# Attention with a mixture of experts on Trainium2: token rows and gate logits out of one matrix product

## The chip, the cores and the metric

The kernel runs on one core of one Trainium2 chip. The metric is the device time of one execution in microseconds (us). Each core has TensorE (PE; its weight loads are shown as PEld), VectorE (DVE), ScalarE (ACT), GpSimd (POOL) and SyncE (SP, which issues DMAs).

## What is computed

```python
scores = scale * q @ k.T            # B=2, H=8, S=576, D=64, f32
# heads 0-3: 0 <= i-j < 32 ; heads 4-7: i >= j and i % 32 == j % 32
attn = softmax(where(mask, scores, -1e9))
x = (attn @ v) -> rows of 512      # 1152 tokens
logits = x @ w_gate                 # 8 experts
e = argmax(logits); gate = softmax(logits)[e]
out_e = relu(x @ w1[e]) @ w2[e]     # per token, experts of capacity 288
y = gate * out_e
h = y @ w_in; out = max(0.01*h, h) @ w_out
```

A token's place with its expert is its rank among the tokens of that expert.

## The kernel before, in words

**Stages.** First the attention with the choice of experts, then the experts (eight, in order of how full they are), then the last two layers. All engines work through lists whose order is written out by hand: the scheduler keeps each engine's order as the program states it.

**Units.** The attention is cut into 16 units (b, c, g): batch b, pair of heads c (c = 2 and 3 are strided heads, c = 0 and 1 local ones) and half g. In a batch the order is (2,0) (2,1) (3,0) (3,1) (0,0) (1,0) (0,1) (1,1). The steps of a unit are named by letters: 0 and 1 are the score products of its two heads (`stage_a`, L471), m the maximum and its subtraction (VectorE, L495), f or F the exp (ScalarE), s the sum and reciprocal (VectorE, three instructions), p the scaling (GpSimd), c the transposes of the weights (L523), e the two copies of them to SBUF (ScalarE, L531), d the product by V (L538) and x the copy of the result to `xT` (ScalarE, L554): features on the partitions, tokens along the row. t is a step that transposes q or k of a later unit and copies it (q in two copies, k in one).

**The loop.** `LOOP` (L23) has a line for each iteration `it`, with the order of the steps: unit `it` is in its steps 0, 1, m, f; unit `it`-1 in F, s, p; unit `it`-2 in c, e, d, x. The letters A, B and C advance the steps behind the units (`advance`, L736): every unit that completes a set of columns of `xT` puts a chain (L748) on a list, and the chain has a triple of actions for each following iteration, one for A, one for B, one for C.

**Behind the units.** Tokens are handled in tiles of 96. `logits` (L617) multiplies a tile of `xT` (stationary) by the 8 columns of the gate (`wg`, moving), for 3 or 6 tiles into one PSUM bank, and VectorE adds the result to `lga`. `rows` (L630) transposes three tiles of `xT` into a bank by the identity, and ScalarE copies them to `xra`, the rows of tokens. In a chain the products of `logits` stand at A and the add at B; `rows` stands at C of the next iteration, its transposes and its copy together; chains with six tiles have two such iterations. When the logits of 288 tokens are complete, `route_idx` (L639) finds their experts and ranks: five small VectorE operations, then ranking products on TensorE, then six more VectorE operations. `scatter` (L705) writes the rows to their places by an indirect DMA of GpSimd.

**Banks.** `bank_t` (L568) gives one of four PSUM banks with the tag T. It serves c (two banks), d, t, `logits`, `rows` and the ranking products. A bank is given out again when its last reader is done.

**The tail.** The last units, v = (1,0,0), w = (1,1,0), y = (1,0,1) and z = (1,1,1), and what is left of the chains are worked through by the string `TAIL` (L42): a step and a unit (`cw` is c of w, `mz0` is m of the first head of z), or a generator, advanced to its next yield. `Lk`, `Lv` and `Lw` are logits, `Rj` to `Rw` are rows, `Ly`, `Lz`, `Ry` and `Rz` the late forms for y and z, `i2` and `i3` the routing of the last two groups, `o` the order of the experts. `wg` is loaded by SP behind the attention's first loads (L723); at the start GpSimd clears `zt` (L379), `qz` and `ets` (L386).

Of the kernel before, what the change touches and what calls it, by code (L numbers as in the profile page):

```python
# [8 lines left out]
F32 = mybir.dt.float32  # L9
# [5 lines left out]
ALU = mybir.AluOpType  # L15
# [24 lines left out]


TAIL = """  # L42
sw ay0 pw ay1 cv my Rk Lk ev r1 dv xv az0 az1 Rk fy cw ew Lv Lk Rj dw cy Rj mz0 xw Lv Rv ey Rv Rl Lw Rl mz1 fz0
fz1 sy Lw i2 dy i2 cz0 xy i2 Rw i2 i2 cz1 sz0 ez0 i2 ez1 Ly i2 dz0 i2 Rw dz1 xz Ly i2 sz1 Ly i2 g5 Ry Lz Lz Lz
i3 i2 i2 i3 g6 i3 Rz Ry i3 Rz g7 wz1 i3 i3 Wy wz0 i3 i3 g8 i3 i3 g9 i3 i3 o g10 g11 G N
"""
FILL_AT = {3: (0, 1), 4: (2, 3), 5: (4, 5), 6: (6, 7)}
# [3 lines left out]
def kernel(ctx, tc, q, k, v, w_gate, w1, w2, w_in, w_out, out, cap):  # L51
    nc = tc.nc
    B, H, S, D = q.shape
    NT, DM = out.shape
    E = w_gate.shape[1]
# [3 lines left out]
    KD = DM // 128  # L59
    NF = FE // 128  # L60
    NG = FF // 128
    TT = 96
    TB = S // TT
# [13 lines left out]
    const = ctx.enter_context(tc.tile_pool(name="const", bufs=1))  # L77
# [145 lines left out]
    make_identity(nc, ident)  # L223
    identb = const.tile([128, 128], BF16, name="identb")
    nc.vector.tensor_copy(out=identb, in_=ident)
    wg = const.tile([128, KD, E], F32, name="wg")
    wgp = const.tile([128, 2, 2, E], F32, name="wgp")
    NI = S // STRIDE
    NR = RS // NI
# [12 lines left out]
    for t, off in ((slice(0, 1), 0), (slice(1, 3), STRIDE)):  # L242
        n = t.stop - t.start
# [119 lines left out]
    def run(gen, n=99):  # L363
        for _ in range(n):
            next(gen, None)

    with ExitStack() as actx:
# [7 lines left out]
            nc.gpsimd.memset(room[:, r:r + 1], float(2 * NT - WR[r]))  # L375
        index = xp.tile([1, E], F32, name="index")
        nc.gpsimd.iota(index, pattern=[[1, E]], base=0, channel_multiplier=0, allow_small_or_imprecise_dtypes=True)
        zt = wts.tile([TT, DM], F32, tag="tmp", name="zt", bufs=3)
        nc.gpsimd.memset(zt, 0.0)  # L379
        H2 = H // 2  # L380
# [187 lines left out]
        def bank_t():  # L568
            if tail[0]:
                tail[0] += 1  # L570
            return bank("S", 2)[:, 0] if tail[0] % 4 > 1 else bank("T")
# [5 lines left out]
        def late_logits(u):  # L577
            b, c, g = u
            pt = bank_t()
            lg = pt[:TT, :6 * E].rearrange("p (t h e) -> p t h e", t=3, h=2)  # L580
            for t in range(3):
                nc.tensor.matmul(lg[:, t], xT[b, c][:, (3 * g + t) * TT:(3 * g + t + 1) * TT], wgp[:, c],
                                 start=True, stop=True)
            yield
            lt = att.tile([TT, 3, 2, E], F32, tag="lt", name="lt", bufs=2)
            for h, r_ in inv(u):
                nc.vector.tensor_tensor(out=lt[:, :, h], in0=lg[:, :, h],
                                        in1=r_.to_broadcast([TT, 3, h.stop - h.start, E]), op=ALU.mult)
            yield
            dst = lga[b][:, 3 * g:3 * g + 3]  # L590
            for h in range(2):
                nc.vector.tensor_tensor(out=dst, in0=lt[:, :, h], in1=dst, op=ALU.add)
# [19 lines left out]
        def xra_of(r):  # L612
            if r not in xra:
                xra[r] = wts.tile([TT, 3, DM], F32, tag="xra", name="xra", bufs=3)
            return xra[r]

        def logits(b, c, t0, n):  # L617
            pt = bank_t()
            lg = pt[:TT, :n * E].rearrange("p (t e) -> p t e", t=n)
            for t in range(n):  # L620
                nc.tensor.matmul(lg[:, t], xT[b, c][:, (t0 + t) * TT:(t0 + t + 1) * TT], wg[:, c],
                                 start=True, stop=True)
            yield
            if c == order[0]:
                lga[b] = att.tile([TT, TB, E], F32, tag="lga", name="lga", bufs=1)
                nc.vector.tensor_copy(out=lga[b][:, t0:t0 + n], in_=lg)
            else:
                nc.vector.tensor_tensor(out=lga[b][:, t0:t0 + n], in0=lg, in1=lga[b][:, t0:t0 + n], op=ALU.add)

        def rows(b, c, t0):  # L630
            pt = bank_t()
            for t in range(3):
                nc.tensor.transpose(pt[:TT, t * 128:(t + 1) * 128],
                                    xT[b, c][:, (t0 + t) * TT:(t0 + t + 1) * TT], ident)
            yield
            nc.scalar.copy(out=xra_of(2 * b + t0 // 3)[:, :, c * 128:(c + 1) * 128],
                           in_=pt[:TT, :384].rearrange("p (t d) -> p t d", t=3))

        def route_idx(r):  # L639
            G = 3  # L640
# [75 lines left out]
        with tc.manual_schedule():  # L716
# [3 lines left out]
            load_vs(0, 1)  # L720
            load_ql(0, (1,))
            load_vl(0)
            nc.sync.dma_start(out=wg, in_=w_gate.rearrange("(c p) e -> p c e", p=128))  # L723
            for f in t_steps(0, order[0]):
                f()
            bg = []
# [20 lines left out]

            def chain(u):  # L748
                b, c, g = u
                if c >= H2 // 2:  # L750
                    lg = logits(b, c, 0, TB)
                    return [[lambda: run(lg, 1), lambda: run(lg)], [nop, nop, lambda: run(rows(b, c, 0))],
                            [nop, nop, lambda: run(rows(b, c, 3))]]
                lg = logits(b, c, 3 * g, 3)
                out = [[lambda: run(lg, 1), lambda: run(lg)], [nop, nop, lambda: run(rows(b, c, 3 * g))]]
                if c == 1:
                    r = 2 * b + g
                    idx, sc = route_idx(r), [lambda t=t: scatter(t) for t in range(3 * r, 3 * r + 3)]
                    out[1][1] = lambda: run(idx, 5)
                    out += [[lambda: run(idx, 1), lambda: run(idx)], [sc[0], nop, sc[1]], [sc[2], lambda: gate(r)]]  # L760
                return out

            def gate(r):
                route_gate(*st.pop(("rt", r)), slice(3 * r, 3 * r + 3), att)
# [14 lines left out]
            for it in range(NU - 2):  # L779
                us = todo.get(it, [])  # L780
                cur, prev = units[it], units[it - 1] if it else None
                for op in LOOP[it].split():
                    if op in "01":
                        stage_a(cur, int(op))
                    elif op in "ABC":
                        advance("ABC".index(op))
                    elif op == "t":
                        steps()
                    elif op == "m":
                        stage_m(cur)  # L790
                    elif op == "f":
                        exp_once(cur)
                    elif op == "F":
                        exp_once(prev)
                    elif op == "s":
                        if prev:
                            run(stage_s(prev))
                    elif op == "p":
                        if prev and prev not in late:
                            stage_p(prev, nc.gpsimd)  # L800
                    elif op == "L":
                        if it == 1:
                            load_qs(1)
                        fill(FILL_AT.get(it, ()))
                        if it == 5:
                            nc.gpsimd.memset(wgp, 0.0)
                            for par in range(2):
                                hp = slice(64 * par, 64 * par + 64)
                                nc.gpsimd.tensor_copy(out=wgp[hp, :, par], in_=wg[hp, :2])
                        if it == 6:  # L810
                            load_vs(1, 0)
                            load_vs(1, 1)
                        if it == 8:
                            load_ql(1)
                        if it == 10:
                            load_vl(1)
                        if it > 8:
                            load_whole(it - 9)
                        if it == NU - 3:
                            for j in range(2 * NE, 2 * NE + NW):  # L820
                                load_wide(j)
                    elif op in "cedx":
                        for u in us:
                            if op == "e":
                                stage_e(u, nc.scalar)
                            else:
                                {"c": stage_c, "d": stage_d, "x": stage_x}[op](u)
                for u in us:
                    if (u[1] < H2 // 2 or u[2] == 1):
                        bg.append(chain(u))  # L830
            bg.clear()
            last = dict(zip("vwyz", units[-4:]))
            gens = {"Lk": logits(1, 3, 0, TB), "Rj": rows(1, 2, 3), "Rk": rows(1, 3, 0), "Rl": rows(1, 3, 3),
                    "Lv": logits(1, 0, 0, 3), "Lw": logits(1, 1, 0, 3), "Ly": late_logits(y), "Lz": late_logits(z),
                    "Rv": rows(1, 0, 0), "Rw": rows(1, 1, 0), "Ry": late_rows(y), "Rz": late_rows(z),
                    "i2": route_idx(2), "i3": route_idx(3)}
            half = {"": both, "0": h0, "1": h1}
# [307 lines left out]
```

## Time and profile before

| what | value |
| --- | --- |
| median of 3 runs | 456.99 us (455.37 to 457.37) |
| profiled execution | 456.36 us, span 454.6 us |
| PE busy | 426.9 us, 94% of the span |
| DVE, ACT, POOL busy | 209.8, 158.5, 69.4 us |
| attention loop and tail | first 85 us or so of the span |
| experts | from about 100 to 234 us |
| last two layers | from 234 us to the end |
| mean granted TensorE clock | 0.974 of full speed |

The profile is of one execution, taken by the hardware. The span goes from the first to the last instruction; the execution's own time is 1.8 us more. A row of the timeline gives the start and the length of an instruction (or of several alike in a row, with their count), its engine, its line in the code, output and inputs; in square brackets stands how long the engine had been idle and what ended that. Matmuls overlap, so that the distance between the starts of two groups tells better than their lengths what one of them costs.

### The profile page before, as it was taken

What the parts mean: (1) busy time and instruction counts of PE and PEld (TensorE: products, weight loads), DVE (VectorE), ACT (ScalarE), POOL (GpSimd) and SP (SyncE); (2) the same over time, 40 slices, a digit from 0 to 9 for tenths busy, and PEclk for the clock granted to TensorE, in tenths of its full rate; (3) what the DMA queues carried; (4) which work ended last, traced back from release to release, by engine and by line L of the source; (5) the groups of instructions that cost most, each with busy time, mean ns of one, the idle gap of its engine ahead of it and who ended that gap; (6) DMA issues with size and microseconds to landing.
All of it is one profiled execution on the core that took longest, in us unless ns stands there. A gap on an engine that the chain in (4) does not pass through costs nothing.

```text
span 454.6 us, 7859 instructions
## 1 busy us (share of the span) xinstructions
PE 426.9 (94%) x2980; PEld 398.1 (88%) x2980; DVE 209.8 (46%) x472; ACT 158.5 (35%) x379; POOL 69.4 (15%) x127
## 2 busy tenths in 40 slices
PE   5999999159999999999999999999999999999994
PEld 5899999129999999999998989989988998998893
DVE  5677878849684442100002788773222233222220
ACT  4777776114232222211112443343322224322222
POOL 6353542730000000550000000000200000200002
PEclk9999999659999999999999999999999999999998
DMA  7999694369779999999980144200100000100001
GB/s 178 216 316 237 199 401 151 107 203 281 237 239 329 354 299 329 303 274 235 298 276 3 48 139 110 77 1 0 71 0 1 0 1 0 69 1 0 2 1 69
DMA packets 56487, 68.85 MB, mean 151 GB/s; under 512 B 20057, under 2 KB 36441, under 8 KB 56441
## 3 DMA queue, kind: packets, MB, share of 16 engines
q1 hardware_dynamic: 53403, 61.34, 44.8%
q0 software_dynamic: 1872, 4.73, 3.0%
q10 hardware_dynamic: 1166, 2.20, 1.7%
q8 instruction: 25, 0.41, 0.4%
q14 instruction: 21, 0.17, 0.1%
HBM read 60.38 MB, written 7.87 MB: 150 GB/s over the span
## 4 chain that ended last, share of the span: by engine, by line
issue 44%; PE 29%; POOL 2%; DMA 1%; POOLq 0%; SPq 0%
PE psS L898 14%; PE psL L905 14%; POOL out_dram L1114 2%; DMA tb<-tab 1%; PE psT L891 1%; PE psL L891 0%; POOLq L1141 0%; POOL gap L697 0%; SPq L123 0%; SPq L121 0%; POOLq L1114 0%; SPq L1060 0%
## 5 line engine op out<-in xcount | busy, mean ns | idle before, releaser
L905 PE MATMUL psL<-ht,pair 128*128 128x128 f32 (+6 forms) x512 | 79.8, 300 | 0.0
L898 PE MATMUL psS<-xe,pair 128*128 128x128 f32 (+6 forms) x512 | 79.2, 299 | 0.0
L898 PEld LDWEIGHTS psS<-xe,pair 128*128 128x128 f32 x512 | 73.0, 193 | 0.0
L905 PEld LDWEIGHTS psL<-ht,pair 128*128 128x128 f32 x512 | 70.7, 190 | 0.5
L1089 DVE TENSOR_TENSOR r<-psS,r 128x384 f32<-128x384 f32 x48 | 26.7, 557 | 82.6 <-ACT r L1088 82.6
L899 ACT ACTIVATE ht<-psS 128x128 f32<-128x128 f32 (+6 forms) x64 | 19.1, 301 | 102.1 <-PE psS L898 93.3
L1088 ACT ACTIVATE r<-psS 128x384 f32<-128x384 f32 x48 | 23.6, 492 | 86.7 <-PE psS L1086 86.6
L1114 POOL DMA_INDIRECT out_dram<-o,tb x9 | 8.7, 965 | 235.7 <-ACT o L1113 234.9
L914 DVE TENSOR_TENSOR yT<-psL,yT 128x128 f32 (+6 forms) x32 | 9.1, 321 | 74.2 <-PE psL L905 54.0
L1092 DVE TENSOR_TENSOR g<-r,g 128x384 fp32r<-128x384 f32 x48 | 26.8, 559 | 27.8 <-ACT g L1091 27.8
L1091 ACT CAST g<-r 128x384 fp32r<-128x384 f32 x48 | 24.6, 513 | 31.7 <-DVE r L1089 31.7
L1083 PE MATMUL psS<-yc,hle 128*128 128x384 f32 x72 | 24.5, 340 | 1.0 <-ACT yc L926 1.0
L490 PE MATMUL psS<-kT,qz 128*72 128x72 f32 (+1 forms) x224 | 24.8, 254 | 0.0
L1084 PE MATMUL psS<-yc,hle 128*128 128x384 f32 x72 | 24.4, 339 | 0.0
L490 PEld LDWEIGHTS psS<-kT,qz 128*72 128x72 f32 (+1 forms) x224 | 23.9, 160 | 0.0
L500 DVE TENSOR_REDUCE mx<-psS 72x8 f32<-72x576 f32 (+2 forms) x17 | 13.5, 795 | 8.1 <-PE psS L490 8.1
L1106 PE MATMUL psL<-hlx,g 128*128 128x512 f32 x42 | 16.6, 396 | 0.0
L1105 PE MATMUL psL<-hlx,g 128*128 128x512 f32 x42 | 16.6, 395 | 0.0
L1104 PE MATMUL psL<-hlx,g 128*128 128x512 f32 x42 | 16.3, 389 | 0.0
L1084 PE MATMUL psS<-yc,hlx 128*128 128x384 f32 x48 | 16.3, 340 | 0.0
L1084 PE MATMUL psS<-yc,hl 128*128 128x384 f32 x48 | 16.3, 340 | 0.0
L1083 PE MATMUL psS<-yc,hlx 128*128 128x384 f32 x48 | 16.1, 336 | 0.0
(309 smaller groups left out, 841.8 us busy)
## 6 DMA issues: line engine op xcount, KB each, us to landing
pair<-in_moe_w_dram SPq DMA_DIRECT2D x64, 512.0 KB
wide<-in_moe_w_out_dram SPq DMA_DIRECT2D x12, 512.0 KB
wide<-in_moe_w_in_dram SPq DMA_DIRECT2D x10, 512.0 KB
xs<-zt SPq DMA_DIRECT2D x8, 384.0 KB
whole<-in_moe_w_in_dram SPq DMA_DIRECT2D x3, 1024.0 KB
whole<-in_moe_w_out_dram SPq DMA_DIRECT2D x2, 1024.0 KB
vl<-in_v_dram SPq DMA_DIRECT2D x12, 128.0 KB
qs<-in_q_dram SPq DMA_DIRECT2D x4, 288.0 KB
```

The source lines that it names most:

```text
L490: nc.tensor.matmul(sv[:, n], lq, lk, start=False, stop=(n == nt - 1))
L898: nc.tensor.matmul(pt[:, :Wx], w[:, c, fs], xe[:, c, :Wx], start=(c == 0), stop=(c == KD - 1))
L899: nc.scalar.activation(out=ht[:, :Wx], in_=pt[:, :Wx], func=ACTF.Relu)
L905: nc.tensor.matmul(acc[n][:, :Wx], w[:, m % 2, n * 128:(n + 1) * 128], ht[:, :Wx], start=(m == 0), stop=(m == NF - 1))
L1083: nc.tensor.matmul(pt[:, :CS], wi[:, 0, c, fs], yc[c][:, 0], start=(c == 0), stop=False)
L1084: nc.tensor.matmul(pt[:, :CS], wi[:, 1, c, fs], yc[c][:, 0], start=False, stop=False)
L1088: nc.scalar.activation(out=r, in_=pt[:, :CS], func=ACTF.Copy, scale=0.01)
L1089: nc.vector.tensor_tensor(out=r, in0=pt[:, :CS], in1=r, op=ALU.max)
L1091: nc.scalar.copy(out=g[:, 0], in_=r)
L1092: nc.vector.tensor_tensor(out=g[:, 1], in0=r, in1=g[:, 0].bitcast(F32), op=ALU.subtract)
L1105: nc.tensor.matmul(accs[ch][s], g[:, 0, ss], wo[:, 1, k % 2], start=False, stop=False)
L1114: apart(lambda: nc.gpsimd.indirect_dma_start(out=out, out_offset=bass.IndirectOffsetOnAxis(ap=tb[:, t, 0:1].bitcast(I32), axis=0), in_=o, ...
```

## The change

The 128 x 128 identity and the 8 columns of the gate lie side by side in one tile, `rx`, for each of the four blocks of features. `rows` multiplies a tile of `xT` by these 136 columns as an ordinary f32 product, for three tiles into one bank; VectorE adds the last 8 columns to `lga`, and ScalarE copies the first 128 to `xra`. `logits` is gone. In a chain the product stands at A, the add at B and the copy at C of one iteration; a strided pair of heads takes two iterations for its six tiles. In the tail the tokens of `logits` are gone and each `R` is advanced three times. `LOOP` is as it was, and so are the late forms for y and z. At the start GpSimd copies the identity four times into `rx`, ahead of clearing `zt`.

```diff
 TAIL = """
-sw ay0 pw ay1 cv my Rk Lk ev r1 dv xv az0 az1 Rk fy cw ew Lv Lk Rj dw cy Rj mz0 xw Lv Rv ey Rv Rl Lw Rl mz1 fz0
-fz1 sy Lw i2 dy i2 cz0 xy i2 Rw i2 i2 cz1 sz0 ez0 i2 ez1 Ly i2 dz0 i2 Rw dz1 xz Ly i2 sz1 Ly i2 g5 Ry Lz Lz Lz
+sw ay0 pw ay1 cv my Rk ev r1 dv xv az0 az1 Rk fy cw ew Rk Rl dw cy Rl mz0 xw Rv Rv ey Rv Rl Rw Rw mz1 fz0
+fz1 sy i2 dy i2 cz0 xy i2 Rw i2 i2 cz1 sz0 ez0 i2 ez1 Ly i2 dz0 i2 Rw dz1 xz Ly i2 sz1 Ly i2 g5 Ry Lz Lz Lz
...
-    wg = const.tile([128, KD, E], F32, name="wg")
...
+        rx = xp.tile([128, KD, 128 + E], F32, name="rx")
+        nc.gpsimd.tensor_copy(out=rx[:, :, :128], in_=ident.unsqueeze(1).to_broadcast([128, KD, 128]))
         zt = wts.tile([TT, DM], F32, tag="tmp", name="zt", bufs=3)
...
-        def logits(b, c, t0, n):
...
+        def rows(b, c, t0):
+            pt = bank_t()[:TT, :3 * (128 + E)].rearrange("p (t f) -> p t f", t=3)
+            for t in range(3):
+                nc.tensor.matmul(pt[:, t], xT[b, c][:, (t0 + t) * TT:(t0 + t + 1) * TT], rx[:, c], start=True, stop=True)
+            yield
+            lg = pt[:, :, 128:]
             if c == order[0]:
-                lga[b] = att.tile([TT, TB, E], F32, tag="lga", name="lga", bufs=1)
-                nc.vector.tensor_copy(out=lga[b][:, t0:t0 + n], in_=lg)
+                if t0 == 0:
+                    lga[b] = att.tile([TT, TB, E], F32, tag="lga", name="lga", bufs=1)
+                nc.vector.tensor_copy(out=lga[b][:, t0:t0 + 3], in_=lg)
             else:
-                nc.vector.tensor_tensor(out=lga[b][:, t0:t0 + n], in0=lg, in1=lga[b][:, t0:t0 + n], op=ALU.add)
-
-        def rows(b, c, t0):
-            pt = bank_t()
-            for t in range(3):
-                nc.tensor.transpose(pt[:TT, t * 128:(t + 1) * 128],
-                                    xT[b, c][:, (t0 + t) * TT:(t0 + t + 1) * TT], ident)
-            yield
-            nc.scalar.copy(out=xra_of(2 * b + t0 // 3)[:, :, c * 128:(c + 1) * 128],
-                           in_=pt[:TT, :384].rearrange("p (t d) -> p t d", t=3))
+                nc.vector.tensor_tensor(out=lga[b][:, t0:t0 + 3], in0=lg, in1=lga[b][:, t0:t0 + 3], op=ALU.add)
+            yield
+            nc.scalar.copy(out=xra_of(2 * b + t0 // 3)[:, :, c * 128:(c + 1) * 128], in_=pt[:, :, :128])
...
-            nc.sync.dma_start(out=wg, in_=w_gate.rearrange("(c p) e -> p c e", p=128))
+            nc.sync.dma_start(out=rx[:, :, 128:], in_=w_gate.rearrange("(c p) e -> p c e", p=128))
...
             def chain(u):
                 b, c, g = u
-                if c >= H2 // 2:
-                    lg = logits(b, c, 0, TB)
-                    return [[lambda: run(lg, 1), lambda: run(lg)], [nop, nop, lambda: run(rows(b, c, 0))],
-                            [nop, nop, lambda: run(rows(b, c, 3))]]
-                lg = logits(b, c, 3 * g, 3)
-                out = [[lambda: run(lg, 1), lambda: run(lg)], [nop, nop, lambda: run(rows(b, c, 3 * g))]]
+                gens = [rows(b, c, t0) for t0 in ((0, 3) if c >= H2 // 2 else (3 * g,))]
+                out = [[lambda r=r: run(r, 1), lambda r=r: run(r, 1), lambda r=r: run(r)] for r in gens]
                 if c == 1:
                     r = 2 * b + g
                     idx, sc = route_idx(r), [lambda t=t: scatter(t) for t in range(3 * r, 3 * r + 3)]
-                    out[1][1] = lambda: run(idx, 5)
-                    out += [[lambda: run(idx, 1), lambda: run(idx)], [sc[0], nop, sc[1]], [sc[2], lambda: gate(r)]]
+                    out += [[nop, lambda: run(idx, 5)], [lambda: run(idx, 1), lambda: run(idx)], [sc[0], nop, sc[1]], [sc[2], lambda: gate(r)]]
                 return out
```

## Rows read from the trace of the kernel before

**Rows 1.** Busy time by stretch: us, PE, PEld, DVE, ACT, POOL (instructions), clock, DMA, GB/s
```profile
16.00:65.60 49.60, 49.50 (x613) 46.34 (x612) 38.30 (x94) 36.57 (x89) 21.66 (x27) 1.00 0.92 272
65.60:81.00 15.40, 15.32 (x169) 14.26 (x168) 11.74 (x44) 10.35 (x26) 4.92 (x8) 1.00 0.47 181
...
100.00:234.00 134.00, 133.92 (x979) 132.20 (x980) 50.02 (x110) 34.40 (x110) 13.48 (x25) 0.99 0.93 289
```

**Rows 2.** Groups of instructions by line and shape, first 185 us
```profile
L621 PE MATMUL psT<-wg,xT 128*96 128x8 f32 x84 | 8.2, 224 | 0.0
...
L633 PE MATMUL psT<-ident,xT 128*96 128x128 f32 x42 | 6.8, 278 | 0.0
...
L636 ACT COPY xra<-psT 96x384 f32<-96x384 f32 x14 | 6.5, 477 | 1.3 <-PE psT L633 1.3
...
L628 DVE TENSOR_TENSOR lga<-psT,lga 96x24 f32<-96x24 f32 x6 | 1.0, 166 | 0.3 <-PE psT L621 0.3
```

**Rows 3.** TensorE in order of time: start us, us, engine, line
```profile
66.59 0.82 PE L490 MATMUL psS<-kT,qz 128*96 128x128 f32 x6
67.24 0.66 PE L529 MATMUL psT<-ident,ex 96*128 96x96 f32 x6
67.74 0.49 PE L633 MATMUL psT<-ident,xT 128*96 128x128 f32 x3
68.07 1.11 PE L621 MATMUL psT<-wg,xT 128*96 128x8 f32 x12
69.10 0.93 PE L551 MATMUL psT<-et,vl 128*64 128x96 f32 x12
...
200.21 1.14 PE L898 MATMUL psS<-xe,pair 128*128 128x144 f32 x8
201.19 1.14 PE L905 MATMUL psL<-ht,pair 128*128 128x144 f32 x8
```

**Rows 4.** All engines in order of time, iteration 7
```profile
37.26 0.69 PE L529 MATMUL psT<-ident,ex 96*128 96x96 f32 x6
...
37.84 0.53 PE L633 MATMUL psT<-ident,xT 128*96 128x128 f32 x3
...
38.30 0.78 PEld L551 LDWEIGHTS psT<-et,vl 128*64 128x64 f32 x12 [0.18 <-ACT et L535]
```

**Rows 5.** All engines in order of time, iteration 11
```profile
53.99 0.67 PE L529 MATMUL psT<-ident,ex 72*72 72x72 f32 x8
...
55.41 0.87 PEld L551 LDWEIGHTS psT<-et,vs 128*64 128x64 f32 x16 [0.18 <-ACT et L535]
```

**Rows 6.** All engines in order of time, iteration 5
```profile
27.24 0.41 PE L441 MATMUL psT<-ident,ql 96*128 96x96 f32 x3
...
28.96 1.02 PE L551 MATMUL psT<-et,vs 128*64 128x72 f32 x16
```

**Rows 7.** All engines in order of time, the tail
```profile
73.06 0.54 DVE L500 TENSOR_REDUCE mx<-psS 96x3 f32<-96x384 f32 x1
...
74.11 0.94 DVE L513 TENSOR_REDUCE s__1281<-ex 96x6 f32<-96x768 f32 x1
...
75.29 0.18 DVE L517 RECIPROCAL s__1281<-s__1281 96x6 f32<-96x6 f32 x1
...
75.74 0.18 DVE L628 TENSOR_TENSOR lga<-psT,lga 96x24 f32<-96x24 f32 x1 [0.27 <-PE psT L621]
...
76.80 0.18 DVE L661 TENSOR_TENSOR oh<-vt,vm 96x24 bf16<-96x24 f32 x1
...
77.38 0.29 PE L665 MATMUL psT<-c,ident 96*96 96x48 f32 x2
```

**Rows 8.** All engines in order of time, the start
```profile
7.33 0.52 POOL L379 MEMSET zt<- 96x512 f32 x1
...
8.05 2.04 POOL L386 MEMSET qz<- 128x1152 f32 x2
...
10.54 0.39 ACT L453 COPY qz<-psT 64x288 f32<-64x288 f32 x1 [2.19 <-PE psT L446]
```

More of the change, by code (lines that the diff above doesn't have):

```diff
@@ L615, in xra_of @@
             return xra[r]
-        def logits(b, c, t0, n):
-            pt = bank_t()
[L619 to L622, printed above, removed]
+        def rows(b, c, t0):
+            pt = bank_t()[:TT, :3 * (128 + E)].rearrange("p (t f) -> p t f", t=3)
+            for t in range(3):
+                nc.tensor.matmul(pt[:, t], xT[b, c][:, (t0 + t) * TT:(t0 + t + 1) * TT], rx[:, c], start=True, stop=True)
             yield
+            lg = pt[:, :, 128:]
             if c == order[0]:
-                lga[b] = att.tile([TT, TB, E], F32, tag="lga", name="lga", bufs=1)
-                nc.vector.tensor_copy(out=lga[b][:, t0:t0 + n], in_=lg)
-            else:
-                nc.vector.tensor_tensor(out=lga[b][:, t0:t0 + n], in0=lg, in1=lga[b][:, t0:t0 + n], op=ALU.add)
-        def rows(b, c, t0):
-            pt = bank_t()
-            for t in range(3):
-                nc.tensor.transpose(pt[:TT, t * 128:(t + 1) * 128],
-                                    xT[b, c][:, (t0 + t) * TT:(t0 + t + 1) * TT], ident)
+                if t0 == 0:
+                    lga[b] = att.tile([TT, TB, E], F32, tag="lga", name="lga", bufs=1)
+                nc.vector.tensor_copy(out=lga[b][:, t0:t0 + 3], in_=lg)
+            else:
+                nc.vector.tensor_tensor(out=lga[b][:, t0:t0 + 3], in0=lg, in1=lga[b][:, t0:t0 + 3], op=ALU.add)
             yield
-            nc.scalar.copy(out=xra_of(2 * b + t0 // 3)[:, :, c * 128:(c + 1) * 128],
-                           in_=pt[:TT, :384].rearrange("p (t d) -> p t d", t=3))
+            nc.scalar.copy(out=xra_of(2 * b + t0 // 3)[:, :, c * 128:(c + 1) * 128], in_=pt[:, :, :128])
         def route_idx(r):
@@ L808 @@
                                 hp = slice(64 * par, 64 * par + 64)
-                                nc.gpsimd.tensor_copy(out=wgp[hp, :, par], in_=wg[hp, :2])
+                                nc.gpsimd.tensor_copy(out=wgp[hp, :, par], in_=rx[hp, :2, 128:])
                         if it == 6:
@@ L832 @@
             last = dict(zip("vwyz", units[-4:]))
-            gens = {"Lk": logits(1, 3, 0, TB), "Rj": rows(1, 2, 3), "Rk": rows(1, 3, 0), "Rl": rows(1, 3, 3),
-                    "Lv": logits(1, 0, 0, 3), "Lw": logits(1, 1, 0, 3), "Ly": late_logits(y), "Lz": late_logits(z),
+            gens = {"Rk": rows(1, 3, 0), "Rl": rows(1, 3, 3),
+                    "Ly": late_logits(y), "Lz": late_logits(z),
                     "Rv": rows(1, 0, 0), "Rw": rows(1, 1, 0), "Ry": late_rows(y), "Rz": late_rows(z),
```

## The prediction

> **What bounds the kernel now.** I first read the busy times of the engines by stretch, to find the stage in which the changed steps lie and the engine that is full there. TensorE is busy for 49.50 of 49.60 us of the attention loop and for 15.32 of 15.40 us of the tail behind it, and again for 133.92 of 134.00 us of the expert stage [rows 1]. So a microsecond of TensorE time taken out of the attention counts, if nothing else becomes late there, and what the attention ends earlier the expert stage starts earlier. VectorE has 38.30 us of work in the loop and 11.74 of 15.40 us in the tail, ScalarE 10.35 there [rows 1]: full enough that a wait put ahead of a long operation is not always made good. Then I read the groups of instructions by shape [rows 2], the row of TensorE in order of time for what one instruction really takes [rows 3], and last the order of all engines in a few iterations and in the tail, where the steps change places.
>
> **What an instruction costs.** Durations of matmuls overlap, so I go by distances between starts. Six f32 products of 128 columns take 0.65 us, 108 ns apiece; three transposes of 128 columns take 0.33 us, 110 ns apiece, one instruction each; twelve logit products (6 tiles, two instructions each) take 1.03 us, 86 ns apiece for 8 columns; eight products of 144 columns in the expert stage take 0.98 us, 122 ns apiece [rows 3]. An f32 product by 136 columns is in none of the rows; it lies between those of 128 and 144 columns, so I take 115 ns, with 108 and 122 as its ends.
>
> **The merged product.** For three tiles the old pair was 6 x 86 + 330 = 846 ns; the new one is 6 x 115 = 690 ns. There are 14 such groups (84 logit products, 42 transposes, 14 copies [rows 2]), 4 of them in the new tail and 10 in the loop. Old work of the loop: 60 products and 9 groups of transposes, 5.16 + 2.97 = 8.1 us; new work 10 x 0.69 = 6.9 us; so TensorE is relieved by 1.2 us in the loop (one group has moved from the tail into it). The ends of the price are worth 0.6 us either way over all 84 products.
> The row shows a transpose at one instruction where a product is two of the same length [rows 3]. The Trainium skill (Perfetto Trace Analysis, Transposes) says that a logical transpose should be a transpose instruction and not an ordinary matmul, because it skips the arithmetic. By that rule alone the sum would be 42 more instructions of 115 ns, 4.8 us more; by the rows the 84 logit products, which load the same tiles again, go away against it.
>
> **The steps that move in the loop.** The transposes stood at step C, mostly between a unit's transposes of its weights (c) and its product by V (d). The new product stands at A, usually ahead of c. The product d needs ScalarE's copy e of what c made, and the transposes covered that wait. In the iteration with c at 37.26 (it = 7) d starts at 38.30, 1.04 us later, and its weight load still waited for the copy [rows 4]; with c at 53.99 (it = 11) the distance is 1.42 us, again ended by the copy [rows 5]. So d comes no sooner than 1.04 to 1.42 us after c. Without the transposes c's own 0.5 us is followed by nothing in it = 7 and 8, a gap of 0.5 to 0.9 us; in it = 7 the transposes left 0.1 of it [rows 4], so 0.4 to 0.8 is new. In it = 5 a step t goes ahead of c and its two copies stand before e on ScalarE: d follows t by 1.72 us, from 27.24 to 28.96 [rows 6], of which t, c and t fill 1.0. There and in it = 8 a part of the gap exists already, so I put 0.1 to 0.4 us each; in it = 9 and 11 other work fills about 1 us, so 0 to 0.25 each. In the other iterations A stands apart from c and d, and nothing is exposed. Together 0.6 to 2.1 us of new gaps; I take 1.0, because it = 7, the iteration with the least cover, shows the small distance. The loop comes to -1.2 + 1.0 = -0.2 us, bounds -1.2 (all gaps filled) and +0.9.
>
> **The tail.** TensorE has less to do here as well: up to the last of the logits that i2 needs, 24 products and 4 groups of transposes, 3.4 us, against 4 x 0.69 = 2.8 us. Of these 0.6 us I give back 0.15 for the wait of Rv for a bank, so the last product, Rw, ends 0.45 us sooner than its counterpart. But VectorE's order is now Rl's add, mz0, Rv's add, Rw's add, mz1, sy, i2; before, mz1 and sy came ahead of the last add. There mz1 ran from 73.06 to 74.11 and sy from there to 75.47, while TensorE was still on the way to the product whose add came at 75.74 and ended at 75.92; the five steps of i2 ended at 76.98, and the ranking products that need them started at 77.38 [rows 7]. Now mz1 and sy are queued behind an add that waits for Rw: that add ends near 75.47 in the same frame, mz1 takes 1.05 us, sy 1.36, i2 1.06, so i2 is ready at about 78.95 and the ranking products start at 79.1 instead of 77.38, 1.7 us later. Behind these on TensorE's queue stand y's late logits, z's product, its late logits, i3, the order of the experts, and with that everything up to the expert stage; nothing there is idle enough to take 1.7 us back. The second half of z's exp on ScalarE, and its copies, wait with mz1, but they are done by then. Bounds: +0.9, if Rw comes 0.8 us earlier than I place it, and +2.2, if its bank waits for one more copy of 0.48 us [rows 2].
>
> **What costs nothing.** The four more adds on VectorE take 0.17 us each [rows 2] beside a full TensorE; without that cover 0.7 us. The new copy of the identity on GpSimd stands ahead of the clearing of zt, which takes 0.52 us for as many columns [rows 8]; as it also reads, I estimate it at 0.5 to 1.0 us. It pushes back the two qz tiles; the first was cleared by about 9.07 and is written at 10.54 [rows 8], so 1.4 us of slack hide it; past that, TensorE's first products would wait. The gate's load on SP has the same descriptors and comes after the attention's own loads, later than that copy. One group of rows is copied an iteration sooner, into a buffer whose scatters left GpSimd's queue an iteration before; that queue keeps its order.
>
> **Sum.** Against the profiled execution (456.36 us, span 454.6 with 1.8 around it; the median of the three runs is 456.99, 0.6 above it and within their scatter): 456.4 - 0.2 + 1.7 = 457.9 us. Its own range, with the 0.6 us of the product's price, is 456.4 - 1.2 - 0.6 + 0.9 to 456.4 + 0.9 + 0.6 + 2.2, that is 455.5 to 460.1.
>
> **Rivals.** (1) *TensorE's saving arrives whole.* If VectorE reaches Rw's add late anyway and the gaps at d are filled, the full difference counts, with the small stalls that stood beside the old transposes (0.46 us for three at 37.84 instead of 0.33 [rows 4], so 0.1 us for ten groups or so): 84 x 0.086 + 14 x 0.33 + 1.0 = 12.8 us, 14 x 0.69 = 9.7 take its place, 3.1 less: 453.3 us. For it speaks the full TensorE [rows 1], against it that d's wait for the copy is on record with the cover still there [rows 4, 5]. Chance 0.15.
> (2) *The banks.* The four PSUM banks of this kind are shared by c (two), d, t and the new product, which keeps its bank from A to C, until both VectorE and ScalarE have read it. If d gets its bank only from the second copy of e, as the 1.42 us of it = 11 suggest [rows 5], each of the five places costs its upper price and Rw waits in the tail too: +0.9 and +2.2 us, 459.5 us. It decides from three of the five places on. Against it speaks the 1.04 us of it = 7 [rows 4]. Chance 0.26.
> (3) *The transposes were the cheap half.* If the logit products cost TensorE nothing, being hidden behind other weight loads, only 42 instructions more remain: 456.4 + 4.8 = 461.2 us. This is where the skill's rule would lead (the Trainium skill, Perfetto Trace Analysis, Transposes). Their 1.03 us for twelve, in a row without gaps, speaks against it [rows 3]. Chance 0.04.
>
> **How the numbers follow.** Half a per cent, 2.3 us, is about what a measurement of this kernel can tell from no change: faster is below 454.7, slower above 459.3. My forecast, the exposed wait in the tail and a loop that comes out about even, has 0.55, and nearly all of its range lies within the band; rival 1 has 0.15 and lies below it; rivals 2 and 3 have 0.30 and lie above it. The range reaches down to the nearer cases of rival 1, 454.6, and up past rival 2, 460.2; it leaves out the far part of rival 1 and rival 3.
>
> **What would show it.** In the changed profile: products of the new line at 115 ns from start to start, 84 of them, and no transposes on the old line; idle time of TensorE's weight loads on V's line until the copy et, above all in it = 5, 7 and 8; VectorE idle ahead of the adds of Rl, Rv and Rw, with mz1 behind them; the ranking products of i2 some 3.6 us after the last add of logits instead of 1.5; the first expert product about 1.5 us later than before. I am wrong if mz1 is not behind Rw's add in time, if the products take over 122 ns or if the tail ends over a microsecond sooner.

## The result, and the profile after

Eight executions of the changed kernel have a median of 461.24 us (459.55 to 463.05), eight of the kernel before on the same chip 457.18 us (455.37 to 459.57): a ratio of 1.0094 [1.007, 1.0118]. The change is slower by 0.9%, 4.1 us. I had forecast 457.9 us, no measurable change, with 460.2 as the upper end. The profiled execution of the changed kernel took 461.29 us, close to its median. The head of its page:

```profile
span 459.6 us, 7782 instructions
...
PE 427.7 (93%) x2938; PEld 397.4 (86%) x2938; DVE 208.5 (45%) x476; ACT 159.1 (35%) x379; POOL 70.4 (15%) x128
```

There are 77 instructions fewer, yet the span is 5.0 us longer than before. The busy times by stretch, in the columns of [rows 1], loop, tail and expert stage:

```profile
16.00:68.50 52.50, 49.82 (x590) 46.20 (x588) 37.82 (x97) 36.82 (x90) 22.39 (x27) 1.00 0.96 272
68.50:85.50 17.00, 15.45 (x153) 13.81 (x152) 12.04 (x45) 10.20 (x25) 4.31 (x8) 0.97 0.36 134
104.40:234.00 129.60, 127.59 (x929) 125.10 (x928) 49.24 (x106) 33.51 (x105) 13.47 (x25) 1.00 0.95 290
```

In the loop TensorE was idle for 0.1 us before [rows 1]; now it is for 2.7 of 52.5 us. In the tail 0.1 us has become 1.6, and in the expert stage 0.1 has become 2.0. The granted clock is full in the loop both times. So TensorE has not become slower; it waits. What it and the others wait for, by groups of line and shape:

```profile
L622 PE MATMUL psT<-rx,xT 128*96 128x136 f32 x84 | 12.1, 283 | 1.3 <-DVE ohs L685 0.7 <-ACT xT L561 0.6
...
L632 ACT COPY xra<-psT 96x384 f32<-96x384 f32 x14 | 6.5, 477 | 5.7 <-DVE lga L630 3.5 <-DVE lga L628 2.1
L552 PEld LDWEIGHTS psT<-et,vl 128*64 128x64 f32 x96 | 6.1, 136 | 1.8 <-ACT et L536 1.4 <-issue 0.2
...
L630 DVE TENSOR_TENSOR lga<-psT,lga 96x24 f32<-96x24 f32 x10 | 1.6, 166 | 2.6 <-PE psT L622 2.6
```

The line to look at is the second. The copies of rows on ScalarE, the same fourteen as in [rows 2], had 1.3 us of idle time ahead of them, ended by TensorE. Now they have 5.7 us, and **VectorE's add ends it**. One such place in order of time, all engines, iteration 7 (the counterpart of [rows 4]):

```profile
38.29 0.66 PE L530 MATMUL psT<-ident,ex 96*128 96x96 f32 x6
38.76 0.94 DVE L514 TENSOR_REDUCE s__631<-ex 96x6 f32<-96x768 f32 x1
...
39.25 1.01 PE L552 MATMUL psT<-et,vl 128*64 128x96 f32 x12 [0.30 <-ACT et L536]
...
40.04 0.23 DVE L630 TENSOR_TENSOR lga<-psT,lga 96x24 f32<-96x24 f32 x2
...
40.21 0.86 ACT L632 COPY xra<-psT 96x384 f32<-96x384 f32 x2 [0.71 <-DVE lga L630]
...
40.96 0.85 ACT L507 ACTIVATE ex<-ex 96x768 f32<-96x768 f32 x1
...
41.71 0.39 ACT L561 COPY xT<-psT 128x288 f32<-128x288 f32 x1
...
42.15 0.94 PE L622 MATMUL psT<-rx,xT 128*96 128x136 f32 x6 [0.59 <-ACT xT L561]
```

The new products of this iteration were through when c started at 38.29. Their add stands on VectorE behind the sum s (38.76), so it comes at 40.04. The copy out of the same bank is held until then, with 0.71 us of idle time on ScalarE; behind it wait the exp (40.96) and x (41.71), and TensorE, whose next product needs x, stands still for 0.59 us. The distance from c to d, 0.96 us, shows the other loss, the one I had expected: d waits for e. The costliest place is iteration 13, in the same view:

```profile
62.46 0.92 PE L622 MATMUL psT<-rx,xT 128*96 128x136 f32 x6
...
64.49 0.17 DVE L628 COPY lga<-psT 96x24 f32<-96x24 f32 x1
...
64.61 0.91 PE L622 MATMUL psT<-rx,xT 128*96 128x136 f32 x6 [0.73 <-DVE ohs L685]
...
64.69 0.48 ACT L632 COPY xra<-psT 96x384 f32<-96x384 f32 x1 [1.81 <-DVE lga L628]
```

Here the logits' step on VectorE is queued behind the small operations of a routing, 64.49 being two microseconds after the product. ScalarE stands still for 1.81 us, and the next product of the line waits 0.73 us, by its row until the routing's last operation on VectorE is done; the bank that is due to it is the routing's.

The tail, VectorE alone, to be held against [rows 7]:

```profile
75.42 0.18 DVE L630 TENSOR_TENSOR lga<-psT,lga 96x24 f32<-96x24 f32 x1 [1.11 <-PE psT L622]
...
77.71 0.18 DVE L630 TENSOR_TENSOR lga<-psT,lga 96x24 f32<-96x24 f32 x1 [0.99 <-PE psT L622]
...
78.40 0.18 DVE L630 TENSOR_TENSOR lga<-psT,lga 96x24 f32<-96x24 f32 x1 [0.52 <-PE psT L622]
78.50 0.54 DVE L501 TENSOR_REDUCE mx<-psS 96x3 f32<-96x384 f32 x1
...
79.55 0.94 DVE L514 TENSOR_REDUCE s__1239<-ex 96x6 f32<-96x768 f32 x1
...
81.63 0.18 DVE L656 TENSOR_TENSOR oh<-vt,vm 96x24 bf16<-96x24 f32 x1
```

VectorE stands idle ahead of the adds of Rl, Rv and Rw, and mz1 and sy follow the last of them, as forecast. To compare kernels I use three marks on TensorE: the first product by V of iteration 2, from which I count the loop; the first score product of y, where the tail begins; and the first ranking product of i2 that needs the experts found (oh, tri). After, and behind it before:

```profile
16.42 1.02 PE L552 MATMUL psT<-et,vs 128*64 128x72 f32 x16
...
68.53 0.36 PE L480 MATMUL psS<-lm,identb 128*96 128x384 bf16 x1
...
81.86 0.18 PE L661 MATMUL psT<-oh,tri 96*96 96x48 bf16 x1 [0.97 <-DVE oh L656]
```

```profile
16.18 1.02 PE L551 MATMUL psT<-et,vs 128*64 128x72 f32 x16
...
65.61 0.33 PE L479 MATMUL psS<-lm,identb 128*96 128x384 bf16 x1
...
77.51 0.19 PE L666 MATMUL psT<-oh,tri 96*96 96x48 bf16 x1
```

The tail, from the second mark to the third, takes 13.33 us for 11.90, so it lost 1.43 us. The loop, from the first mark to the second, takes 52.11 us for 49.43: 2.68 us lost.

### The profile page after: what moved, and what is told of

It is laid out like the page before. It is cut to its first block, busy times and chain, and to the rows that moved or that the text cites. A ratio compares the mean times of both kernels' runs of the same rounds, so it can differ in the third digit from the quotient of the medians.

```text
span 459.6 us, 7782 instructions
## 1 busy us (share of the span) xinstructions
PE 427.7 (93%) x2938; PEld 397.4 (86%) x2938; DVE 208.5 (45%) x476; ACT 159.1 (35%) x379; POOL 70.4 (15%) x128
## 4 chain that ended last, share of the span: by engine, by line
issue 44%; PE 25%; DMA 5%; POOL 2%; SPq 1%; POOLq 0%
PE psL L895 13%; PE psS L888 12%; DMA xr<-xs 2%; DMA pair<-in_moe_w_dram 2%; POOL out_dram L1104 2%; PE psT L881 1%; DMA tb<-tab 1%; SPq L123 0%; SPq L121 0%; POOLq L1131 0%; POOL gap L692 0%; POOLq L1104 0%; SPq L875 0%; SPq L1050 0%
```

## The experiments

Each was timed against the kernel before in five rounds; "loop" and "tail" are the two stretches just defined, read from the run's own profile, and the changed kernel has 52.11 and 13.33 by them.

**The tail's order alone.** The loop stays as changed; in the tail mz0, mz1 and sy go ahead of the adds that they stood behind.

```diff
-... Rk Rl dw cy Rl mz0 xw Rv Rv ey Rv Rl Rw Rw mz1 fz0
-fz1 sy i2 dy i2 ...
+... Rk Rl dw cy mz0 Rl xw Rv mz1 Rv ey Rv Rl Rw fz0
+fz1 sy Rw i2 dy i2 ...
```

> The tail re-dealt alone: mz1 ahead of Rv's add on VectorE, sy ahead of Rw's; the loop as changed. Theory T (VectorE's order in the tail costs 1.4 us, the ranking products of i2 come 13.3 us after the tail's first score product instead of 11.8): the distance falls to about 12, time 459.8. Theory S (ScalarE's copy waits for VectorE's add, and that alone sets the loss): the tail stays as long, 461.2. Theory C (d has lost its cover): no change either, 461.2.

Measured: tail 11.81 us, so the 1.5 us come back. In the whole time nearly nothing of it is seen: 462.94 us, 1.0079 [1.0046, 1.0111], though the interval leaves room for the 0.3% that I expected. In this profile, of an execution of 464.51 us, the experts wait 5.2 us for their pairs of weights, 1.6 in that of the changed kernel.

**The order of the two readers in the loop.** In the loop's generators, the copy goes ahead of the add, both at C; the tail stays as changed.

```diff
-            nc.vector.tensor_tensor(out=lga[b][:, t0:t0 + 3], in0=lg, in1=lga[b][:, t0:t0 + 3], op=ALU.add)
             yield
             nc.scalar.copy(out=xra_of(2 * b + t0 // 3)[:, :, c * 128:(c + 1) * 128], in_=pt[:, :, :128])
+            nc.vector.tensor_tensor(out=lga[b][:, t0:t0 + 3], in0=lg, in1=lga[b][:, t0:t0 + 3], op=ALU.add)
```

> In the loop the two readers of a bank change places: at C first ScalarE's copy, then VectorE's add, which now waits for the copy instead of the other way round; tail as changed. Theory S: ScalarE no longer idles 5.6 us for adds ahead of its copies, the step A waits less for x, the tail's first score product comes at 66.5 instead of 68.5, time 459.2. Theory C: TensorE still waits for e ahead of d in the iterations 5, 7 and 8 by 0.3 to 0.5 us each, the tail starts at 68.5 as before, 461.2. Theory T: nothing changes, 461.2.

> Both edits: the tail re-dealt, and copy ahead of add in the loop. If S and T are separate costs they add: 461.2 - 2.0 - 1.4 = 457.8, the old time. If one hides the other, it is no better than the better of the two single edits, 459.2 to 459.8.

Measured: with the readers exchanged 461.73 us, 1.0034 [1.0006, 1.0063], and with the tail's order besides 459.50 us, 1.0014 [0.9982, 1.0046]. By the profile of the second the loop is 50.37 us (from 15.98), 1.74 less than changed, and the tail 11.80 us; in the profile of the first the loop is 50.37 us as well, with a tail of 13.34. The ends of the second's tail:

```profile
66.35 0.36 PE L480 MATMUL psS<-lm,identb 128*96 128x384 bf16 x1
...
78.15 0.18 PE L668 MATMUL psT<-oh,tri 96*96 96x48 bf16 x1
```

So the order of the readers and the tail's order together make up most of the loss: without them the kernel can't be told from the one before. These runs and the first experiment's shared a chip. With the tail re-dealt both times, exchanging the readers took the ratio there from 1.0079 to 1.0014, 0.65% or 3.0 us. The loop shows 1.6 of it (51.99 to 50.37 us); the rest lies behind the attention and is not explained.

**The product back at C.** To give d its cover back, the product and its copy stand at C, where the transposes were, and the add comes at A of the next iteration; the tail has the better order, with the add left over from the loop at its start (Rj).

```diff
-                out = [[lambda r=r: run(r, 1), lambda r=r: run(r, 1), lambda r=r: run(r)] for r in gens]
+                out = [[nop, nop, lambda r=r: run(r, 3)] for r in gens] + [[nop]]
+                for i, r in enumerate(gens):
+                    out[i + 1][0] = lambda r=r: run(r)
```

> The merged product at the place of the old transposes (step C, product and copy together, the add at A of the next iteration), and the tail re-dealt. Theory C: d has its cover again, no gap ahead of it, and TensorE's saving of about 1.2 us in the loop arrives, 455.5 to 456.5, over a microsecond less than copy ahead of add alone. Theory S: the copy waits for no add here as there, so the two come out equal, 457.8. If neither is right it stays near 460.

> The product at step C and the tail re-dealt, once more, because its first profile fell on a low granted clock between 10 and 20 us. If the remaining gaps of the loop were the lost cover (C), the tail starts at 65.3 to 65.6, a microsecond sooner than with copy ahead of add alone (66.35), and the time stands at 0.3% below the kernel before. If not, at 66.4 and level with it.

Measured: 457.79 us, 0.9968 [0.9939, 0.9997], and again on another chip 456.04 us, 0.9958 [0.9931, 0.9985]. In the first profile the mean granted clock was 0.83 of full speed between 10 and 20 us, so I read the second: loop 49.05 us, tail 11.76.

```profile
16.70 1.02 PE L552 MATMUL psT<-et,vs 128*64 128x72 f32 x16
...
65.75 0.33 PE L480 MATMUL psS<-lm,identb 128*96 128x384 bf16 x1
...
77.51 0.18 PE L669 MATMUL psT<-oh,tri 96*96 96x48 bf16 x1
```

The tail starts at 65.75, a little behind the 65.3 to 65.6 that I expected. This version, the better version from here on, beats both kernels: 0.4% faster than before, while the changed kernel in the same session was 0.8% slower:

> The changed kernel again, beside the others on one chip. All theories: 0.9% over the kernel before, the tail's first score product at 68.5 and the ranking products of i2 13.3 us behind it.

Measured: 462.05 us, 1.0081 [1.0043, 1.0119]; the result repeats on a second chip. The tail is 13.34 us as expected. It starts at 69.66 instead of 68.5, but in this profile too the granted clock was 0.83 between 10 and 20 us, so its loop (53.59 us) can't be compared.

**The merged product taken apart again.** The same order of steps, but every tile has its transpose and its products by the gate's columns, in the same bank and places.

```diff
-                nc.tensor.matmul(pt[:, t], xT[...], rx[:, c], start=True, stop=True)
+                nc.tensor.transpose(pt[:, t, :128], xt, ident)
+                nc.tensor.matmul(pt[:, t, 128:], xt, rx[:, c, 128:], start=True, stop=True)
```

> As the run before, with the merged product taken apart again at the same places: three transposes and three products by the gate's 8 columns into the same bank, in the same order, read by the same two instructions. If a group costs 846 ns against 690, as distances between starts had it, the 14 groups cost 2.2 us more, 0.5% over the merged one. If the work of TensorE hardly differs (46.3 against 45.8 us in the loop by the least distances), 0.5 to 1.0 us more. If the rule holds that transposes are the cheaper form, it is faster by some microseconds.

Measured: 455.73 us, 0.9959 [0.9932, 0.9985], loop 49.00, tail 11.73: the same as merged; none of the three expected outcomes came. One group of three tiles and the step after it, on TensorE in order of time, first merged, then apart:

```profile
28.40 0.88 PE L622 MATMUL psT<-rx,xT 128*96 128x136 f32 x6
29.11 0.41 PE L442 MATMUL psT<-ident,ql 96*128 96x96 f32 x3
```

```profile
28.33 0.28 PE L623 MATMUL psT<-ident,xT 128*96 128x128 f32 x1
28.45 0.26 PE L624 MATMUL psT<-rx,xT 128*96 128x8 f32 x2
28.56 0.29 PE L623 MATMUL psT<-ident,xT 128*96 128x128 f32 x1
...
29.05 0.45 PE L442 MATMUL psT<-ident,ql 96*128 96x96 f32 x3
```

0.71 us merged, 0.72 us apart; over the ten groups of the loop, from the start of each to the start of the next step, 7.69 us against 7.55. The idea of the change, one product for two purposes, is worth nothing here; what both versions gain over the kernel before comes from where the steps and the gate's products stand. The rule weighed in the prediction (the Trainium skill, Perfetto Trace Analysis, Transposes) is to use a transpose instruction and not an ordinary matmul; in these two kernels that makes no difference to the time.

**Rl put behind y's product by V in the tail,** to let v and w through earlier.

```diff
-... ew Rk Rl dw cy mz0 Rl xw Rv mz1 Rv ey Rv Rl Rw fz0 fz1 sy Rw i2 dy ...
+... ew Rk Rv dw cy mz0 Rv xw Rw mz1 ey fz0 fz1 Rv sy Rw i2 dy Rl i2 ...
```

> The run with the product at C, and in the tail the group Rl, which i2 does not need, put behind dy as filler, so that Rw and its add come 0.7 us sooner on TensorE. If the tail is bound by the way from Rw's add to the ranking products, these come 11.2 to 11.5 us behind the first score product of the tail instead of 11.8, 0.3 to 0.5 us in the time; if TensorE's work bounds it, nothing.

Measured: 456.57 us, 0.996 [0.9935, 0.9985]. The tail is shorter, 11.29 us, but the stretch from the ranking of i2 to that of i3 takes 5.82 us instead of 4.97. Nothing is gained in the time, where I expected 0.3 to 0.5 us.

**The disputed wait put back by itself.** From the better version, only the order of the two readers in the loop is turned: add, then copy, both at C, where the better version has the add at A of the next iteration. Products and tail are the same; by the program's order a bank is let go earlier than there.

```diff
+            nc.vector.tensor_tensor(out=lga[b][:, t0:t0 + 3], in0=lg, in1=lga[b][:, t0:t0 + 3], op=ALU.add)
             nc.scalar.copy(out=xra_of(2 * b + t0 // 3)[:, :, c * 128:(c + 1) * 128], in_=pt[:, :, :128])
-            yield
-            nc.vector.tensor_tensor(out=lga[b][:, t0:t0 + 3], in0=lg, in1=lga[b][:, t0:t0 + 3], op=ALU.add)
```

> The best version so far (product at C, tail re-dealt) with nothing changed but the order of a bank's two readers in the loop: VectorE's add first, at C, ScalarE's copy behind it. Theory S: the copies on ScalarE's queue wait for the adds, which stand behind m and s on VectorE; with that x, t's copies and e come late, and TensorE's loop ends 1.5 to 3 us later (tail's first score product at 67.3 to 68.8 instead of 65.75), 0.3 to 0.6% more time. If the order of the readers had nothing to do with it, nothing changes: 65.75, 0.4% below the kernel before.

Measured: 457.61 us, 1.0026 [1.0005, 1.0048], against 0.9958 [0.9931, 0.9985] with the copy first, each beside the kernel before on its own chip; the intervals stand apart. The two chips differ by themselves (the kernel before took 456.93 us on this one, 458.17 on the other), so the price in the whole time is less sure than that in the loop: 0.7% by the ratios, 0.3% by the medians as they are. The loop is 50.94 us (15.76 to 66.70) for 49.05, the tail 11.77, unchanged. The tail starts a little ahead of the expected 67.3 because the loop began 0.94 us earlier. The waits of the loop (us in total, times, longest), first with the add first, then with the copy first:

```profile
ACT xra L636 <- DVE lga L632: 5.0, 5, 1.8
...
ACT xra L636 <- DVE lga L630: 2.5, 3, 1.8
```

```profile
ACT xra L637 <- PE psT L622: 2.1, 5, 0.8
...
DVE lga L632 <- ACT xra L637: 0.2, 1, 0.2
```

With the add first ScalarE's copies wait 7.5 us for VectorE. With the copy first VectorE's add waits 0.2 us for ScalarE, and the copies wait for TensorE alone. Where it reaches TensorE, in order of time with the add first:

```profile
39.26 0.23 DVE L632 TENSOR_TENSOR lga<-psT,lga 96x24 f32<-96x24 f32 x2
...
39.43 0.85 ACT L636 COPY xra<-psT 96x384 f32<-96x384 f32 x2 [1.61 <-DVE lga L632]
...
41.20 0.41 ACT L452 COPY kT<-psT 128x288 f32<-128x288 f32 x1
...
41.66 0.74 PE L491 MATMUL psS<-kT,qz 128*72 128x72 f32 x8 [1.11 <-ACT kT L452]
```

The copy of k is late behind the held copy, and TensorE waits 1.11 us for it.

**The changed tail put back by itself,** from the better version (the diff is that of the first experiment, undone).

> The product at C in the loop, with the tail of the changed kernel. Theory T: the loop ends at 65.75 as in the run with the tail re-dealt, the ranking products of i2 come 13.3 us behind the tail's first score product instead of 11.8, and the time is 0.2 to 0.35% above that run, about level with the kernel before. If the tail's cost came only from a late loop, the distance stays 11.8.

Measured: 457.42 us, 1.0018 [0.9998, 1.0037], loop 49.05 as in the better version, tail 13.30:

```profile
64.69 0.33 PE L480 MATMUL psS<-lm,identb 128*96 128x384 bf16 x1
...
77.99 0.18 PE L669 MATMUL psT<-oh,tri 96*96 96x48 bf16 x1 [0.97 <-DVE oh L664]
```

Its interval and that of the better version stand apart as well. The tail's order costs 1.5 us at the ranking products. In the whole time its price is not settled: 0.6% by these ratios, again from two chips, 0.3% by the medians, and 0.15 and 0.2% in the two pairs of the first experiments, less than their intervals can tell.

## Why the prediction was wrong

**The step that failed** is "What costs nothing". There the four more adds on VectorE were taken as free beside a full TensorE, which they are as work. But I costed only VectorE's side, and not what waits for an add. Add and copy now read the same bank, and the program lets the second reader wait for the first: in the rows ScalarE's copy is released by VectorE's add. In the kernel before each of the two had a bank to itself. So every add that is late on VectorE holds up ScalarE's queue, with the exp, e, x and t in it, and through these TensorE. The prediction named the two readers only under its second rival, as the reason why the bank is held long. The price by itself is shown by the run with the wait put back: 1.9 us of the loop (50.94 - 49.05) and a higher ratio; exchanging the readers in the changed kernel gave 1.74 us back. The Trainium skill (PSUM — Partial Sum Buffer, PSUM bank collisions raise a hardware error) says that two different engines must not access one bank in the same quarter of its partitions at the same time, two readers included, and that the hardware does not arbitrate. The waits agree with a program ordered that way; no run here has the two reading together.

**The other terms,** against the working in the prediction:

- *The merged product.* I took 115 ns, 108 to 122. Where the next step follows at once, six start 0.69 to 0.71 us ahead of it (28.40 to 29.11 above), 115 to 118 ns apiece. Right.
- *The old logit products.* I took 86 ns apiece from twelve in a row. Six in the loop of before took 0.48 us, 80 ns apiece:

```profile
40.40 0.62 PE L621 MATMUL psT<-wg,xT 128*96 128x8 f32 x6
40.88 0.29 PE L479 MATMUL psS<-sm,identb 128*72 128x288 bf16 x1
```

The shortest distance for six is 0.45 us, 75 ns apiece. By the shortest distances the old steps of the loop cost 60 x 75 + 27 x 108 ns = 7.4 us and the new ones 60 x 115 ns = 6.9: a saving of 0.5 us, not 1.2. By the distances as they stand, each from the start of a group to the start of the next step, with whatever TensorE waited beside it, they cost 8.79 us before, 7.52 in the changed kernel and 7.69 in the better version: a saving of 1.1 to 1.3. In the better version 0.4 us arrives; there the transposes of step t take 0.6 us more than before (7.11 for 6.54). So the rows do not settle the size of this term by itself.
- *The lost cover at d*, taken at 1.0 us (0.6 to 2.1), was right. In the version with copy ahead of add and the product at A, TensorE takes longer than before from the starts of the transposes c to the starts of the next steps by 0.55, 0.38 and 0.31 us in the iterations 5, 7 and 8, three of the places that I had named: 1.24 us. (In iteration 5 the waiting step is t, behind ScalarE's copy of q.) The distance from c to d in iteration 7, 0.96 us, is a little under the 1.04 that I used.
- *The bank in iteration 13* had no term. The same distance grows by 0.79 us there; the product behind c waits for the routing's bank.
- *The tail*, taken at 1.7 us (0.9 to 2.2), was right in mechanism and size: 1.43 us, confirmed from both sides (1.5 us back in the first experiment, 1.5 us lost in the last).

For the loop I forecast -1.2 + 1.0 = -0.2 us, +0.9 at most. The version with the readers exchanged, which has these two terms and not the held copy, is 0.94 us above the kernel before (50.37 against 49.43): 1.1 us more than my sum, most of it the wait in iteration 13. The add ahead of the copy brings the other 1.74 us of the measured +2.68, and has no term in my sum either. Loop and tail together come to +4.1 us where I forecast +1.5.

**The rivals.** TensorE's saving did not arrive whole. The banks were the nearest of the rivals: one place shows the wait for a bank (0.73 us ahead of the product of iteration 13), but d waits for its copy, not for a bank, and the better version, which by its order holds a bank until the add of the next iteration, is faster than the one with the wait put back, which lets it go at C. Rival 3 gave 461.2 us, the measured time, by a wrong mechanism and so by luck: the kernel with the transposes back in it is as fast as the one with merged products.

**What stays open.** The ranking products of i3 start 3.6 us later than before (86.86, before 83.23): the loop and tail give 4.1 us, the late start of the loop 0.24, and the stretch between the two rankings gives 0.7 back. The 0.24 us arise early, where TensorE waits for the load of k until 6.11 us (before 5.87). The rest of the 5.0 us by which the span is longer lies behind. The first expert product starts 3.0 us later (104.44 for 101.41), and then the experts wait for weights, by the changed kernel's costliest groups:

```profile
L888 PE MATMUL psS<-xe,pair 128*128 128x128 f32 (+6 forms) x512 | 78.7, 297 | 1.6 <-DMA pair<-in_moe_w_dram 1.6
```

Before and in the better version that wait is absent, with the first experiment it is 5.2 us. It is not lateness alone: the version with both orders exchanged waits 2.3 us, and its first expert product starts at 101.11, earlier than before. All four profiles from the chip of the first experiments have the wait (2.3 to 6.2 us); on the other chips only the changed kernel has it. No run isolates it. It may be why the first experiment's tail gained 1.5 us and its time hardly anything. The new copy of the identity at the start cost nothing: it took 0.60 us of GpSimd (my estimate was 0.5 to 1.0), the first qz tile was cleared by about 9.6 and written at 10.78, by a copy that waited for TensorE and not for GpSimd.

## What to carry to other kernels

When two results are put into one bank, list the readers of that bank: here the second waited for the first in program order, so it inherits the lateness of the first one's queue; let the engine with the fuller schedule of dependants read first, and give the other the late place. When steps of other work cover a wait, moving them is a cost even if they get cheaper. And before merging two kinds of instruction to save TensorE time, measure the small ones where they stand between others, not in the longest row.

## What the runs showed that I had not expected

Products by 8 columns between transposes of the same tiles are cheaper than in a row of their own: two of them take 0.11 us between two transposes (28.45 to 28.56 above), 55 ns apiece, against 75 to 86 ns. Some of it goes to the transposes beside them, 0.12 to 0.13 us instead of 0.11; with these at 0.11, the products of the group cost 65 ns apiece (0.72 - 0.33 us for six). That is what makes the unmerged version as short as the merged one.

A VectorE operation of 24 elements on 96 partitions (vt, the third of i3's five) took 1.16 us before and 0.18 us in the changed kernel. Before:

```profile
81.59 1.16 DVE L655 SCALAR_TENSOR_TENSOR vt<-gates,c 96x24 f32<-96x24 f32 x1
81.74 0.51 POOL L609 TENSOR_TENSOR xra<-xra,s__1347 96x192 f32<-96x192 f32 x1
82.20 0.51 POOL L609 TENSOR_TENSOR xra<-xra,s__1315 96x192 f32<-96x192 f32 x1
```

GpSimd began to scale rows 0.15 us behind its start. So it is in the version taken apart and in the one with Rl late (1.20 and 1.16 us, GpSimd 0.18 and 0.13 us behind). In the better version GpSimd began 0.21 us behind, and vt took 0.37. The stretch between the two rankings is 5.7 to 5.8 us in those three kernels and 5.0 in the better version and in the changed one, which gave the changed kernel 0.7 us back. A start of GpSimd close behind vt is not enough for it, though: in the changed kernel's i3 GpSimd began 0.14 us behind vt (86.13, 86.27), and vt took 0.18 us; there GpSimd's second scaling took 0.91 us instead of 0.51. And with the changed tail put back vt took 0.18 us, and the fifth operation, oh, 0.82. So the two engines seem to hold each other up, now the one and now the other; the cause was not tested.
